# Linear attention and a four-expert merge: the first token tile and the second batch's attention moved into the seven-product block schedule

## The chip, the core and the metric

The kernel runs on one NeuronCore of a Trainium2 chip. Its engines work through queues of their own, in order: TensorE (PE in the profile) for matrix products, VectorE (DVE), ScalarE (ACT), GpSimd (POOL), and SyncE (SP), which here only issues transfers. PE writes to PSUM, which has eight banks of 512 float32 for each of 128 partitions; ACT and DVE read it. The metric is the device time of one execution in microseconds (us); lower is better. Eight executions of the kernel before had a median of 514.97 us (513.4 to 515.87).

## The reference

```python
phi = lambda x: where(x > 0, x, exp(x) - 1) + 1        # q, k, v: (8, 8, 576, 64)
q_p, k_p = phi(q), phi(k)
kv  = einsum('bhsd,bhse->bhde', k_p, v)
num = einsum('bhsd,bhde->bhse', q_p, kv)
den = einsum('bhsd,bhd->bhs', q_p, k_p.sum(2))[..., None] + 1e-06
x   = (num / den).transpose(0, 2, 1, 3).reshape(4608, 512)

p   = probs / (probs.sum(-1, keepdims=True) + 1e-09)   # (4608, 4)
out = 0
for e in range(4):
    out += p[:, e:e+1] * (maximum(x @ w1[e], 0) @ w2[e])   # w1 512x1024, w2 1024x512
```

All inputs are float32. The kernel computes in float16 with float32 sums.

## The kernel before

**Tiles.** Each batch has 576 tokens. The first 512 of batch j make token tile j (0 to 7); the 64 left over of all eight batches (the "lefts": `rl`, `kl`, `vl`, `ql`, `xl`) make tile 8. A unit (j, e) is one tile through one expert: layer 1 (512 to 1024, relu) and layer 2 (1024 to 512, scaled by the token's probability and added into `acc` by `add_acc`). There are 36 units.

**Two ways to do a unit.** The plain way (`layer1_group` L468, `layer2_part` L522) uses 32 matmuls of 512 columns for each layer. The block way splits each product of matrices 2 by 2 and uses seven half-size products instead of eight: `Block` (L659) does half of a unit's layer 1 in the products p1, p2, p6, p7, p5, p4, p3, each of 4 matmuls of 256 columns, so that a unit's layer 1 is 56 such matmuls; `layer2_product` (L591) does layer 2 in 14 steps of 4 matmuls. The block way needs sums beforehand: of the weights (`weight_sums` L549 for w1 and `weight_sums2` L563 for w2, four DVE operations each per expert, the fourth overwriting a quarter of the weight), of the tokens (`token_sum` L635, four POOL operations per tile into `tt`) and of the hidden values (`hidden_sum` L576, eight POOL operations per unit into `hs`). A block also takes five ACT operations (a copy `pe`, copies `u2` and `u3`, two relus) and two DVE operations (`add_relu` L656, from c22 and p3).

Before, the five units (0,0) to (0,3) and (1,0) are done the plain way and the 31 others in blocks.

**Attention of a batch** (`class Batch` L206). Loads of q, k and v in quarters of 2 heads (`load`, 256 KB) and of the lefts (`load_left`, 64 KB); phi of q and k (`phi_act` on ACT, `phi_dve` on DVE), cast of v (`vcast`), the products k'v (`kv`, ACT copies into `kvz`), the transposes of q' (`pe_qT` on PE with an ACT or DVE copy, or `dma_qT` by a transfer), the quotients (`nd`, `norm` on DVE), and the transposes of x into `xT` (`pe_xT` or `dma_xT`). Batches 0 and 1 take phi in one ACT and two DVE operations; later ones take two ACT operations (1+x, and exp into PSUM) and one DVE operation.

**Order.** Everything is in a manual schedule: each engine works in the order in which the program issues. First comes batch 0's attention, with the GpSimd queue issuing all weights (`load_w` L163: w1 and w2 of expert 0, then of 1, 2, 3, each in halves of 512 KB as float16) and after them batch 1's lefts and quarters (L827 to L830). Then the plain units of tile 0 run as a list of pieces (L891 to L906); `steps` (L855) lays batch 1's attention among the pieces of expert 2's end and expert 3. Then follows layer 1 of (1,0), also plain, and from L928 on the slot loop (L979): in each slot one product of the present or the previous block, and between them what is put at positions in slots: layer 2 products (`L2AT`, `L2ORD`), hidden sums (`HSUM`), and the attention of the next batch (`batch_steps` L740, positions in `ATTN`). Batch 2's attention, which runs beside tile 1, has a table of positions of its own, `ATTN[0]`, packed into 41 slots; the others use `ATTN[1]`, spread over 53. Eight weight sums for experts 2 and 3 lie in tile 1 (`WS2`).

**PSUM.** The tags `s`, `e`, `b` and `py` have two banks each. Blocks use `b` and `e`, layer 2 uses `py`. The attention's PSUM tiles (`aps` L156) take `s` and `e` in turn while tile 0 runs, and `s` alone afterwards (L921). A layer 2 step writes one half of a `py` bank (`run` or `side`).

**Buffers.** `rawb` has six buffers (NRAW) for quarters in flight; `rl` has one.

Of the kernel before, what the change touches and what calls it, by code (L numbers as in the profile page):

```python
# [19 lines left out]
CFG = {  # L20
    "ATTN": (
        dict(
            v=(0.3, 1.0, 3.2, 13.0),
            k=(0.6, 3.0, 6.7, 8.2),
            kd=(5.8, 6.8, 6.8, 9.5),
            lv=6.1,
            lk=9.7,
            lkd=12.0,
            kv=(13.6, 15.8),
            q=(16.1, 17.6, 19.1, 20.5),  # L30
            qd=(16.1, 18.4, 21.0, 22.6),
            lq=23.8,
            lqd=24.3,
            qT=23.8,
            nd=(32.8, 33.3, 34.1, 34.5, 38.2, 38.5),
            nl=41.4,
# [18 lines left out]
    "WS2": (6.6, 9.6, 26.1, 27.5, 25.7, 30.2, 37.6, 43.0),  # L55
# [4 lines left out]
    "TSUM1": (-1.2, 0.1, 0.4, 0.8),  # L60
# [4 lines left out]
def kernel(  # L65
# [11 lines left out]
    ATTN, WS2, HSUM, L2ORD, L2AT, TSUM, TSUM1 = (  # L77
        CFG[x] for x in ("ATTN", "WS2", "HSUM", "L2ORD", "L2AT", "TSUM", "TSUM1")
    )
# [34 lines left out]

    NB2 = 1
# [47 lines left out]
    def load_w(e, r):  # L163

        if e == 0 and r < 4:
            fs = slice(r * F // 4, (r + 1) * F // 4)
            nc.gpsimd.dma_start(out=w1_sb[e][:, :, fs], in_=w1_src[e, :, :, fs])
        elif r < 2 and e > 0:
            ds = slice(r * 2, r * 2 + 2)
            nc.gpsimd.dma_start(out=w1_sb[e][:, ds], in_=w1_src[e, :, ds])  # L170
        else:
            fs = slice(r % 2 * 4, r % 2 * 4 + 4)
            nc.gpsimd.dma_start(out=w2_sb[e][:, fs], in_=w2_src[e, :, fs])
# [32 lines left out]
    class Batch:  # L206
# [5 lines left out]
        def load_left(self, *names, eng=nc.sync):  # L212
            b = self.b
            if "k" in names:
                self.rl = praw.tile([P, 3, HG, D], FP32, tag="rawl", bufs=1, name="rl")
            for i, (name, src) in enumerate((("k", k), ("v", v), ("q", q))):
                for u in range(2):
                    if name in names:
                        eng.dma_start(
                            out=self.rl[u * HP : (u + 1) * HP, i],  # L220
                            in_=src[b, u * HG : (u + 1) * HG, SM:S].rearrange(
                                "h r d -> r h d"
                            ),
                        )

        def load(self, name, i, eng=nc.sync, home=None):
# [9 lines left out]
            else:  # L236
                t = pm.tile(shape, FP32, tag=home, bufs=2 if home == "u2" else 1, name="rawu")
# [6 lines left out]
        def alloc(self):  # L244
            self.kp = pa.tile([P, CM, H, D], FP16, tag="kp", bufs=1, name="kp")
            self.vp = pa.tile([P, CM, H, DE], FP16, tag="vp", bufs=1, name="vp")
            nc.gpsimd.memset(self.vp[:, :, :, D:DE], 1.0 / SX)
            self.vl = pa.tile([P, HG, DE], FP16, tag="vl", bufs=1, name="vl")
            nc.gpsimd.memset(self.vl[:, :, D:DE], 1.0 / SX)
            if self.b < 2:  # L250
# [3 lines left out]
            if self.b < 2:  # L254
                self.x = pm.tile([P, NPAIR, CM, P], FP16, tag="tt", bufs=2, name="x_sb")
            self.xl = pa.tile([P, 2, P], FP16, tag="xsl", bufs=1, name="x_sl")
            if self.b < 2:
# [9 lines left out]
        def phi_act(self, name, i):  # L267

            if self.b >= 2 and (name, i) == ("q", 0):
# [3 lines left out]
            if self.b >= 2:  # L273
# [8 lines left out]
        def phi_dve(self, name, i):  # L282
            src, dst, ee = self.ph.pop((name, i))
            dst, ee = (a.rearrange("p c h d -> p c (h d)") for a in (dst, ee))
            if self.b >= 2:
# [14 lines left out]
        def left_act(self, *names):  # L300

            for name in names:
# [8 lines left out]
                if self.b >= 2:  # L311
# [13 lines left out]
        def left_dve(self, name):  # L325
            src, el, parts = self.ph.pop("l" + name)
            for us, dst in parts:
                if self.b >= 2:
# [22 lines left out]
        def dma_qTl(self):  # L351
            for u in range(2):
# [4 lines left out]
                )  # L357

# [45 lines left out]
        def nd(self, i0, n):  # L404

            if i0 == 0 and self.b >= 2:
# [20 lines left out]
        def nd_left(self):  # L427
# [11 lines left out]
            for u in range(2):  # L439
# [151 lines left out]
    def layer2_product(j, e, hT, hss, p, i):  # L591


        if p == 2:
            pys[i] = new_py()
        run, side = pys[i][:, 0:DH], pys[i][:, DH:Dm]
# [5 lines left out]
            1: (run, lambda k: hT[k // 2][:, k % 2, 0, ts], w[:, lo, 0:DH], False),  # L602
# [32 lines left out]
    def token_sum(j, i):  # L635
# [7 lines left out]
        nc.gpsimd.tensor_tensor(out=t[:, i], in0=a, in1=b, op=AO.subtract)  # L643
# [100 lines left out]
    def batch_steps(bt, nxt, put, at, at_next):  # L744

        mine = order_of(at)
        later = mine + (order_of(at_next) if nxt is not None else [])

# [4 lines left out]
        def load_left():  # L753
            if nxt is not None:
                nxt.load_left("k", "v", "q")
# [7 lines left out]
        put(min(at["v"][0], at["k"][0]) - 0.01, bt.alloc)  # L763
        for m, (n, i) in enumerate(mine):
            if n == "v":
                put(at[n][i], bt.vcast, i)
                put(at[n][i] + 1, load, m + NRAW)
            else:
                put(at[n][i], bt.phi_act, n, i)
                put(at[n + "d"][i], bt.phi_dve, n, i)  # L770
                put(at[n][i] + 1, load, m + NRAW)
# [7 lines left out]
        put(at["lqd"] + 2, bt.dma_qTl)  # L779
        put(at["qT"], bt.dma_qT)  # L780
        for i in range(6):
            put(at["nd"][i], numerators, 3 * i, min(3, NPAIR * CM - 3 * i))
# [12 lines left out]
    with tc.manual_schedule(  # L795
        engines={ENG.PE, ENG.Activation, ENG.DVE, ENG.SP, ENG.Pool}
    ):
        b0.alloc()
        homes = ["h"] * 4 + [None] * NRAW + ["u2", "u3"]
# [22 lines left out]
        for r in range(6):  # L822
            load_w(0, r)
        for e in range(1, E):
            for r in range(4):
                load_w(e, r)
        b1.load_left("k", "v", "q", eng=nc.gpsimd)  # L827
        homes = [None] * NRAW + ["u2", "u3", "u2"] + [None] * 3
        for (n, i), home in zip(ORDER, homes):
            b1.load(n, i, nc.gpsimd, home=home)  # L830
# [24 lines left out]
        steps = [  # L855
            (1, b0.left_q),
            (2, emit_probs),
            (4, b0.dma_qTl),
            (22, b0.nd_left),
            (36, b1.alloc),  # L860
            (46, b1.phi, "q", 0),
            (46, b1.phi, "q", 1),
            (47, b1.left_kv),
            (48, b1.phi, "k", 0),
            (48, b1.phi, "k", 1),
            (49, b1.pe_qT, 0),
            (50, b1.pe_qT, 1),
            (50, b1.vcast, 0),
            (50, b1.vcast, 1),
            (52, b1.kv, 0),  # L870
            (53, b1.phi, "q", 2),
            (53, b1.phi, "q", 3),
            (54, b1.nd_pair, 0),
            (55, b1.phi, "k", 2),
            (55, b1.phi, "k", 3),
            (56, b1.nd_pair, 1),
            (56, b1.vcast, 2),
            (57, b1.pe_qT, 2, nc.scalar),
            (57, b1.vcast, 3),
            (58, b1.pe_xT, 0),  # L880
            (59, b1.pe_qT, 3, nc.scalar),
            (60, b1.kv, 2, 1),
            (60, b1.pe_xT, 1),
            (61, b1.kv, 3, 1),
            (62, b1.nd_pair, 2),
            (63, b1.nd_pair, 3),
        ]
        early = {(1, 1 + 2 * i): (0, i) for i in range(3)}
        early.update({(2, 1 + 2 * i): (1, i) for i in range(4)})
        done = 0  # L890
        pieces = unit(0, 0, hT, phs) + [g for e in range(1, E) for g in unit(0, e)]  # L891
        for i, g in enumerate(pieces):
            g[0](*g[1:])

            e, r = divmod(i, 16)
            if (e, r) in ((2, 14), (2, 15), (3, 1)):
                weight_sums(3, (r + 2) % 4 if e == 2 else 2)
            if r in (9, 11, 13) and e < 3:
                weight_sums(e, r // 2 - 4)
            elif r == 15 and e in (1, 2):  # L900
                weight_sums(e, 3)
            elif r in (1, 3, 5, 7) and (e, r) in early:
                weight_sums2(*early[e, r])
            while done < len(steps) and i >= steps[done][0]:
                steps[done][1](*steps[done][2:])
                done += 1  # L906

        hT = [new_h(), new_h()]
        phs = [layer1_group(1, 0, 0, hT, None, range(0, 2))]
        phs.append(layer1_group(1, 0, 1, hT, None, range(0, 2)))  # L910
        b1.pe_xT(2)
        phs.append(layer1_group(1, 0, 2, hT, None, range(0, 2)))
        b1.pe_xT(3)
        b1.left_q()
        for n, i in order_of(ATTN[0])[0:NRAW]:
            bts[2].load(n, i)
        bts[2].load_left("k", "v", "q")
        b1.dma_qTl()
        for i in range(4):
            token_sum(1, i)  # L920
        turn["aps"], turn["ph"] = ["s"], ["e"]  # L921
        for g in layer1(1, 0, hT, phs):
            g[0](*g[1:])
        weight_sums(0, 3)
        weight_sums(E - 1, 3)


        NSLOT, LAG = 7, 6  # L928
        units = [(j, e) for j in range(1, NTILES) for e in range(E) if (j, e) > (1, 0)]
        nslots = 2 * NSLOT * len(units)  # L930
# [5 lines left out]
        blocks = []  # L936
        for i, g in enumerate(layer2(1, 0, hT, 4)):
            put_at(i * (2 * NSLOT + LAG) // 16 + 0.5, *g)
        put_at(2 * NSLOT + LAG + 0.5, weight_sums2, 0, 3)
        for n, (j, e) in enumerate(units):  # L940
            hT, hss = [None, None], [[None] * 4, [None] * 4]
            blocks += [Block(j, e, d, hT) for d in range(2)]
            at = 2 * NSLOT * (n + 1) + LAG

            def hsum(d, i, hT=hT, hss=hss):
                hidden_sum(hT[d], hss[d], i)

            for d in range(2):
                for i in range(4):
                    put_at(at + HSUM[d][i], hsum, d, i)  # L950
            for m in range(14):
                put_at(at + L2AT[m], layer2_product, j, e, hT, hss, L2ORD[m // 2], m % 2)
# [71 lines left out]
```

## Time and profile before

| | |
|---|---|
| median of eight executions | 514.97 us (513.4 to 515.87) |
| profiled execution | 513.4 us, span 511.6 us, mean TensorE clock 0.991 |
| PE busy | 489.0 us (96%) |
| DVE, POOL, ACT busy | 365.7, 345.7, 323.8 us |
| data moved by transfers | 54.29 MB, mean 106 GB/s |
| time to landing of a 512 KB weight half | 10.6 to 20.8 us, in a queue |

A line of the timeline gives start and duration in us, engine, line of the kernel, operation, what it writes and reads, its shape, how many instructions are merged, and in brackets how long its engine stood idle before it and what ended that. SPq and POOLq are the issuing of transfers. The end of a matmul is modelled with its latency: four matmuls of 256 columns show as 0.60 us but the next four start 0.44 us after them, so lengths of PE work are taken here between starts.

### The profile page before, as it was taken

What the parts mean: (1) busy time and instruction counts of PE and PEld (TensorE: products, weight loads), DVE (VectorE), ACT (ScalarE), POOL (GpSimd) and SP (SyncE); (2) the same over time, 40 slices, a digit from 0 to 9 for tenths busy, and PEclk for the clock granted to TensorE, in tenths of its full rate; (3) what the DMA queues carried; (4) which work ended last, traced back from release to release, by engine and by line L of the source; (5) the groups of instructions that cost most, each with busy time, mean ns of one, the idle gap of its engine ahead of it and who ended that gap; (6) DMA issues with size and microseconds to landing.
All of it is one profiled execution on the core that took longest, in us unless ns stands there. A gap on an engine that the chain in (4) does not pass through costs nothing.

```text
span 511.6 us, 11256 instructions
## 1 busy us (share of the span) xinstructions
PE 489.0 (96%) x4199; PEld 397.1 (78%) x4199; DVE 365.7 (71%) x787; ACT 323.8 (63%) x647; POOL 345.7 (68%) x340
## 2 busy tenths in 40 slices
PE   6899978889999999999999999999999999999994
PEld 3444444567888888898989898888988888888883
DVE  5725585459986878687868796889688756775674
ACT  5753485994689568955895589559954464446520
POOL 2622523055887697769866986698669877987781
PEclk9999999999999999999999999999999999999999
DMA  8999944646444424442445244623231020001003
GB/s 239 209 208 207 218 151 167 180 117 108 64 150 162 97 63 136 148 108 63 140 145 118 50 142 145 108 51 113 84 68 27 2 83 1 1 21 65 1 1 83
DMA packets 80935, 54.29 MB, mean 106 GB/s; under 512 B 46224, under 2 KB 73872, under 8 KB 80880
## 3 DMA queue, kind: packets, MB, share of 16 engines
q1 hardware_dynamic: 71760, 41.64, 31.2%
q0 software_dynamic: 9120, 11.93, 12.0%
q8 instruction: 33, 0.54, 0.4%
q14 instruction: 22, 0.18, 0.1%
HBM read 45.16 MB, written 9.44 MB: 107 GB/s over the span
## 4 chain that ended last, share of the span: by engine, by line
PE 80%; DVE 9%; ACT 5%; DMA 2%; issue 2%; SPq 1%; POOL 0%; DVEq 0%; ACTq 0%; POOLq 0%
PE py L611 35%; PE pb L673 19%; PE pe L673 14%; PE ph L472 5%; PE py L527 5%; DVE acc L518 3%; DVE x_sb L397 2%; PE psum_kv L374 1%; DMA qT<-qp 1%; PE psum_nd L414 1%; DVE h L657 1%; DMA rl<-in_v_dram 1%; ACT u L684 1%; SPq L239 1%; ACT psum_ee L279 1%
## 5 line engine op out<-in xcount | busy, mean ns | idle before, releaser
L518 DVE SCALAR_TENSOR_TENSOR acc<-py,p_sb,acc 128x256 f32<-128x256 f32 (+1 forms) x390 | 184.0, 488 | 62.0 <-PE py L611 48.9
L583 POOL TENSOR_TENSOR hs<-h 128x512 f16<-128x512 f16 x62 | 71.9, 1160 | 67.7 <-DVE h L657 67.7
L657 DVE CUSTOM_DVE_ANT_0 h<-pe,u 128x512 f16<-128x512 f32 x124 | 85.4, 689 | 36.2 <-PE pe L673 18.7
L673 PEld LDWEIGHTS <-w 128*128 128x128 f16 x992 | 96.4, 98 | 16.3 <-issue 2.9
L611 PEld LDWEIGHTS <-h 128*128 128x128 f16 x992 | 97.4, 98 | 14.9 <-issue 2.7
L611 PE MATMUL py<-w,h 128*128 128x256 f16 x744 | 107.4, 274 | 0.7 <-DVE acc L518 0.2
L585 POOL TENSOR_TENSOR hs<-hs,h 128x512 f16<-128x512 f16 x62 | 71.6, 1155 | 24.9 <-PE py L611 22.4
L684 ACT COPY u<-pb 128x512 f32<-128x512 f32 x124 | 73.0, 589 | 22.5 <-PE pb L673 20.2
L611 PEld LDWEIGHTS <-hs 128*128 128x128 f16 x744 | 71.8, 98 | 11.4 <-issue 2.9
L673 PEld LDWEIGHTS <-s 128*128 128x128 f16 x744 | 72.5, 98 | 9.3
L611 PE MATMUL py<-t,hs 128*128 128x256 f16 x496 | 74.4, 272 | 1.2 <-DVE acc L518 1.0
L673 PE MATMUL pb<-tt,w 128*128 128x256 f16 x496 | 74.7, 273 | 0.9 <-ACT u L684 0.9
L589 POOL TENSOR_TENSOR hs<-h,hs 128x512 f16<-128x512 f16 x62 | 71.7, 1156 | 3.2 <-PE py L611 3.2
L587 POOL TENSOR_TENSOR h<-h 128x512 f16<-128x512 f16 x62 | 72.1, 1162 | 0.0
L699 ACT ACTIVATE h<-pe 128x512 f16<-128x512 f32 x62 | 37.0, 597 | 53.1 <-PE pe L673 52.6
L693 ACT COPY pe<-pb 128x512 f32<-128x512 f32 x62 | 35.9, 579 | 46.8 <-PE pb L673 43.2
L527 PE MATMUL py<-w,h 128*128 128x512 f16 x160 | 38.4, 379 | 0.8 <-DVE acc L518 0.8
L472 PE MATMUL ph<-xT,w 128*128 128x512 f16 x160 | 37.1, 379 | 0.8 <-ACT xT L451 0.7
L717 ACT ACTIVATE h<-pb 128x512 f16<-128x512 f32 x62 | 36.9, 596 | 1.4 <-PE pb L673 1.2
L673 PE MATMUL pe<-tt,s 128*128 128x256 f16 x248 | 37.3, 273 | 0.0
L673 PE MATMUL pb<-tt,s 128*128 128x256 f16 x248 | 37.2, 273 | 0.0
L516 ACT ACTIVATE acc<-py,p_sb 128x256 f32<-128x256 f32 (+1 forms) x64 | 31.4, 507 | 7.5 <-PE py L527 4.2
(102 smaller groups left out, 634.7 us busy)
## 6 DMA issues: line engine op xcount, KB each, us to landing
out_dram<-acc SPq DMA_DIRECT2D x32, 256.0 KB, 2.4
w<-in_moe_w_dram POOLq DMA_DIRECT2D x14, 512.0 KB, 19.6
rawb<-in_v_dram SPq DMA_DIRECT2D x26, 256.0 KB, 2.9
rawb<-in_q_dram SPq DMA_DIRECT2D x26, 256.0 KB, 3.0
rawb<-in_k_dram SPq DMA_DIRECT2D x26, 256.0 KB, 2.8
w<-in_moe_w_dram POOLq DMA_DIRECT2D x4, 256.0 KB, 8.0
rawb<-in_v_dram POOLq DMA_DIRECT2D x4, 256.0 KB, 4.4
out_dram<-acc SPq DMA_DIRECT2D x8, 128.0 KB, 2.4
```

Source lines behind the costliest of these rows:

```text
L472: nc.tensor.matmul(out=ph, lhsT=w1_sb[e][:, dc, fj * P : (fj + 1) * P], rhs=xT_of(j)[:, dc], start=(dc == 0), stop=(dc == DC - 1),)
L518: nc.vector.scalar_tensor_tensor(out=acc, in0=ps, scalar=pscal, in1=acc, op0=AO.mult, op1=AO.add)
L527: nc.tensor.matmul(out=py, lhsT=rows(hT, fj)[:, ns * P : (ns + 1) * P], rhs=w2_sb[e][:, fj, :], start=(fj == 0), stop=(fj == FC - 1),)
L583: nc.gpsimd.tensor_tensor(out=hs[0], in0=a21, in1=a22, op=AO.add)
L585: nc.gpsimd.tensor_tensor(out=hs[1], in0=hs[0], in1=a11, op=AO.subtract)
L587: nc.gpsimd.tensor_tensor(out=a21, in0=a11, in1=a21, op=AO.subtract)
L589: nc.gpsimd.tensor_tensor(out=hs[3], in0=a12, in1=hs[1], op=AO.subtract)
L611: nc.tensor.matmul(out=ps, lhsT=lhsT(k), rhs=rhs[:, k], start=first and k == 0, stop=k == FH - 1, skip_group_check=True,)
L657: nc.vector._custom_dve(TENSOR_ADD_SAT, out=out, in0=ps, in1=u, s0=BIG, s1=0.0)
L673: nc.tensor.matmul(out=ps[:, kk], lhsT=lk(kc), rhs=rhs[:, kc], start=first and kk == 0 and kc == 0, stop=kc == 1, skip_group_check=True,)
L684: nc.scalar.copy(u, self.b)
L699: nc.scalar.activation(self.h[:, :, 0, 0:NH], self.e5, AF.Relu)
```

## The change

Layer 1 of (0,1), (0,2), (0,3) and (1,0) and layer 2 of (1,0) are done in blocks; layer 2 of tile 0 stays plain, and (0,0) stays plain altogether. Tile 0's token sums are four DVE operations. The slot loop is gone: every step, from the second half of (0,0)'s layer 1 on, has a position in `CFG`, and the sorted list is issued. Batch 1's attention gets positions 20 to 56 beside the blocks of (0,2) and (0,3), takes phi as the later batches do (two ACT operations, one DVE), keeps its q' and x in the buffers of `kp` and `vp`, and uses only the two `s` banks for all its PSUM tiles. The lefts of batches 0 and 1 are transposed by PE (`pe_qTl`, `pe_xl`) and not by transfers. Batch 2's attention uses the table that the later batches use. The GpSimd queue issues weights and batch 1's quarters and lefts mixed, in the order `DMA`. In the last unit, layer 2's `run` and `side` halves get banks of their own from `b` and `e`, and its steps come in another order.

```diff
 CFG = {
+    "DMA": ('w100', 'w101', 'w102', 'w103', 'w110', 'w200', 'w201', 'w111', 'lk0', 'w210', 'w121', 'w120', 'w211', 'lv0', 'lk1', 'v0', 'lv1', 'w221', 'w220', 'w131', 'lq0', 'k0', 'w130', 'k1', 'v1', 'v2', 'k2', 'lq1', 'k3', 'v3', 'q3', 'q2', 'q0', 'q1', 'w231', 'w230'),
+    "BLK": (-1.0, 6.0, 13.0, 21.0, 28.0, 35.0, 53.0),
+    "L1P": (-40.4, -39.9, -23.1, -21.7, -21.5, -19.6, -16.2, -14.3),
+    "L2P": ((-14.0, -13.2, -12.6, -12.6, -11.8, -5.4, -4.5, -2.9, -1.4, 0.3, 3.9, 5.5, 9.1, 11.6, 16.0, 16.8), (20.4, 21.5, 22.7, 23.0, 23.4, 23.9, 23.9, 24.6, 24.6, 24.7, 27.2, 27.7, 27.8, 28.4, 28.4, 34.6), (37.0, 37.1, 38.8, 40.1, 40.6, 41.8, 42.5, 43.5, 44.6, 45.0, 45.4, 45.9, 46.4, 47.5, 53.3, 55.2), (49.2, 49.8, 55.6, 55.7, 56.7, 57.2, 58.6, 59.2, 61.3, 61.4, 62.1, 62.7, 64.9, 65.9, 67.0, 71.8)),
+    "TS0": (-37.7, -33.9, -28.9, -12.1),
+    "WS1": ((-3.3, -1.0, 7.3, 14.1), (-8.2, -3.1, -1.2, -1.2), (15.2, 16.0, 23.6, 15.3), (27.1, 27.6, 29.5, 27.2)),
+    "WS2": ((6.9, 13.3, 43.3, 50.6), (24.5, 29.9, 35.6, 38.6), (51.7, 61.8, 74.1, 59.6), (63.9, 66.1, 70.6, 80.0)),
     "ATTN": (
         dict(
...
+            v=(22.5, 27.0, 27.3, 31.4),
+            k=(21.5, 26.8, 28.0, 28.3),
+            kd=(26.2, 29.1, 29.3, 29.4),
+            lv=24.5,
+            lk=20.4,
+            lkd=26.4,
+            kv=(31.8, 33.5),
+            q=(34.0, 36.3, 36.6, 39.3),
+            qd=(36.4, 37.8, 38.6, 43.0),
+            lq=28.6,
+            lqd=29.4,
+            qt=(42.4, 43.2, 43.5, 43.6),
+            nd=(43.1, 44.9, 45.7, 46.8),
+            xt=(44.1, 48.8, 49.5, 49.8),
+            qtl=35.1,
+            nl=53.0,
+            xl=55.6,
+            next=(8.5, 35.8, 36.8, 39.6, 43.2, 49.6),
         ),
...
+    def load_first():
+        parts = [x for x in CFG["DMA"] if x[0] in "vkq"]
+        homes = dict(zip(parts, [None] * NRAW + ["acc"] + [None] * 5))
+        b1.alloc_left()
+        for x in CFG["DMA"]:
+            if x[0] == "w":
+                load_w(*map(int, x[1:]))
+            elif x[0] == "l":
+                b1.load_left(x[1], eng=nc.gpsimd, us=(int(x[2]),))
+            else:
+                b1.load(x[0], int(x[1]), nc.gpsimd, home=homes[x])
...
-            if self.b >= 2:
+            if self.b >= 1:
                 nc.scalar.activation(dst.rearrange("p c h d -> p h c d"), src, AF.Identity, bias=1.0)
                 ee = aps([P, HQ * CM * D], FP32, "psum_ee")
...
+        def pe_qTl(self):
+            ps = aps([P, 2, P], FP16, "psum_ql")
+            for a in range(2):
+                nc.tensor.transpose(out=ps[:, a], in_=self.ql[:, 2 * a : 2 * a + 2], identity=identh)
+            for u in range(2):
+                us = slice(u * HP, (u + 1) * HP)
+                nc.scalar.copy(out=self.qTl[:, :, u, us], in_=ps[:, :, us])
...
-        run, side = pys[i][:, 0:DH], pys[i][:, DH:Dm]
+        if (j, e) == (NTILES - 1, E - 1):
+            if p == 2:
+                pys[i] = [ppm.tile([P, DH], FP32, tag=tag, bufs=2, name=f"p{tag}") for tag in ("b", "e")]
+            run, side = pys[i]
+        else:
+            if p == 2:
+                pys[i] = new_py()
+            run, side = pys[i][:, 0:DH], pys[i][:, DH:Dm]
...
-        for r in range(6):
-            load_w(0, r)
-        for e in range(1, E):
-            for r in range(4):
-                load_w(e, r)
-        b1.load_left("k", "v", "q", eng=nc.gpsimd)
...
+        load_first()
...
-        steps = [
-            (1, b0.left_q),
...
+        turn["aps"] = ["s"]
...
+        def put_block(at, *g):
+            bl = Block(*g)
+            for pos, name in ((0, "p1"), (3, "p2"), (5, "p6"), (8, "p7"), (9, "p5"), (9.1, "c22"), (11, "p4"), (13, "p3")):
+                put_at(at + pos, getattr(bl, name))
...
+        for e in range(E):
+            h0 = hT if e == 0 else [None, None]
+            for d in range(2) if e else ():
+                put_block(CFG["BLK"][2 * e - 2 + d], 0, e, d, h0)
+            for i, pos in enumerate(CFG["L2P"][e]):
+                put_at(pos, layer2_part, 0, e, i // 4, h0, i % 4, 4)
+            for i in range(4):
+                put_at(CFG["WS1"][e][i], weight_sums, e, i)
+                put_at(CFG["WS2"][e][i], weight_sums2, e, i)
+        base = CFG["BLK"][6]
...
+            order = L2ORD if n < len(units) - 1 else (2, 1, 5, 6, 3, 7, 4)
...
+                batch_steps(bts[j + 1], nxt, put, ATTN[j > 0], ATTN[1])
...
         work.sort(key=lambda w: w[0:2])
+        for _, _, g in work:
+            g[0](*g[1:])
```

In `DMA`, `w1er` is part r of expert e's w1 and `w2er` of its w2; `lk0` is a half of the lefts of k; `k0` is quarter 0 of k.

## The prediction

> **What bounds the kernel now.** I read the page first: PE is busy 96%, so its work and its gaps are the time. Then the windows, to find the gaps; then the timeline there.
>
> ```profile
> PE   6899978889999999999999999999999999999994
> ...
> 19.40:61.90 42.50, 42.20 (x205) 19.53 (x206) 19.49 (x38) 19.05 (x33) 13.70 (x20) 1.00 1.15 206
> 62.00:91.60 29.60, 25.46 (x166) 13.26 (x165) 19.68 (x51) 19.30 (x40) 10.20 (x16) 1.00 0.54 180
> 91.70:134.80 43.10, 38.08 (x305) 28.66 (x304) 31.32 (x63) 31.24 (x63) 20.42 (x17) 0.96 0.54 114
> 186.80:238.20 51.40, 51.40 (x490) 46.05 (x489) 40.95 (x90) 37.99 (x78) 40.26 (x39) 1.00 0.42 114
> ```
>
> After each stretch and its length come busy us (and instructions) of PE, PEld, DVE, ACT, POOL, then clock, DMA share, GB/s. From 187 on PE has no gap. Up to 62 it hardly has one, but transfers run at a share over 1: weights come as fast as they can. Between 62 and 135 lies the loss.
>
> How much, I count from starts. Four 256-column matmuls follow each other at 0.437 us, four of 512 at 0.864, a small one (128 or 130 columns) takes 0.0575. From 62.0 to 91.6 PE does 98 wide and 68 small ones, 25.1 of 29.6 us: 4.5 lost. The first block of (1,1) starts at 91.73, of (2,0) at 134.83:
>
> ```profile
> 91.73 0.60 PE L673 MATMUL pb<-xT,w 128*128 128x256 f16 x4
> 134.83 0.60 PE L673 MATMUL pb<-xT,w 128*128 128x256 f16 x4
> 186.83 0.60 PE L673 MATMUL pb<-xT,w 128*128 128x256 f16 x4
> 238.25 0.60 PE L673 MATMUL pb<-xT,w 128*128 128x256 f16 x4
> ```
>
> Between the first two lie 152 block matmuls (16.6), (1,0)'s plain layer 2 (6.9), 19 layer 2 steps (8.3) and attention (2.5): 34.3 of 43.1, 8.8 lost. Tile 2 takes 52.0, tile 3 51.4, and their work is 51.4. So 13.3 us can be had here.
>
> **The change, part by part.** *Less PE work.* A layer is 32 x 0.216 = 6.91 plain, 56 x 0.109 = 6.11 in blocks. Five layers change: 4.0 us less. Eight small transposes are new: 0.5 more.
>
> *The new transfer order.* The GpSimd queue lands its transfers one after another:
>
> ```profile
> 30.33 0.70 POOL L170 DMA_DIRECT2D w<-in_moe_w_dram  x1 [2.01 <-DMA w<-in_moe_w_dram]
> 33.02 0.71 POOL L170 DMA_DIRECT2D w<-in_moe_w_dram  x1 [1.99 <-DMA w<-in_moe_w_dram]
> 38.05 0.74 POOL L173 DMA_DIRECT2D w<-in_moe_w_dram  x1 [1.79 <-DMA w<-in_moe_w_dram]
> ```
>
> Each issue plus its time to landing gives, after expert 0's w1, halves at 24.7, 26.4, 29.1, 31.8, 35.2, 37.7, 40.4, 42.8, 45.3, 48.4, 51.0, 53.4, 56.0 and 58.9. Batch 1's quarters then land 0.95 apart, its lefts about 0.25. In the new order v0, five lefts and k0 stand before the twelfth half: k0 lands at 51.0 + 2 x 0.95 + 5 x 0.25 = 54.1 (ends: 51.0 if they ride along free, 57.5 if a quarter costs as much as a half, 2.65; I take the quarters' own rows), w130 at 56.5, k1 to k3 at 57.5 to 61.5, q1 at 66, w230 at 71.5. On its queue lk0 must wait until batch 0's left q is read (near 24); four halves are then under way until 31.8, so nothing runs dry.
>
> *PE up to there.* (0,0) runs as before to 27.6. Waits for w201 (0.6), for batch 0's leftover quotient (0.9) and for w120, before the first block of (0,2) (1.5, to 40.5), leave PE at 53.3 with nothing to do before w130. ACT comes to batch 1's k0 near 46.5 and stands there until 54.1, with two relus behind it that must free a `b` bank before (0,3) can start.
>
> *ACT from 54.1.* Its queue from k0 to the first transpose copy of q' holds 34 operations of 512 columns and nine small ones. In the trace such operations start 0.513 apart (nine from 92.43 to 97.05), though each shows 0.6:
>
> ```profile
> 92.94 0.62 ACT L295 CAST vp<-rawb 128x512 f16<-128x512 f32 x1
> 93.46 0.63 ACT L274 ACTIVATE kp<-rawb 128x512 f16<-128x512 f32 x1
> 93.99 0.59 ACT L279 ACTIVATE psum_ee<-rawb 128x512 f32<-128x512 f32 x1
> 94.51 0.61 ACT L295 CAST vp<-rawb 128x512 f16<-128x512 f32 x1
> ```
>
> 34 x 0.513 + 2.8 for the small ones + 0.5 waiting for k2 is 20.7: the copy ends at 74.8. PE has 20.0 us of work between 56.5 and tile 1, and follows ACT. DVE has 25 us in the 30 (six `add_relu` at 0.69, seven phis at 0.69, ten weight sums at 0.69, five sums into `acc` at 0.74, eight quotients at 0.55), so it runs beside.
>
> *From 74.8 to tile 1.* What is left on PE hangs on that copy: 12 groups at 0.435 (5.2), ten attention groups at 0.23 (2.3), and the hand-overs quotient to DVE to transpose, 1.9. Tile 1 starts at 84.2.
>
> *The clock.* PE idles at half the time between 53 and 66. The trace shows what that can do: the clock was 0.50 from 113.2 to 116.6, after 3.4 us in which PE ran 1.3. A gap of 3.1 us (66.7 to 69.8) did nothing. One slow stretch costs 0 (PE waits for ACT anyway) to 1.7 us (half of 3.41); I take 0.7, since PE reaches the copies only 1.4 us early. So tile 1 starts at 84.9.
>
> ```profile
> 110.00:111.00 1.00, 0.00 (x1) 0.00 (x0) 0.17 (x1) 1.00 (x3) 0.00 (x0) 1.00 0.58 168
> 114.00:115.00 1.00, 1.00 (x7) 0.73 (x5) 0.65 (x2) 1.00 (x3) 1.00 (x2) 0.50 0.39 108
> ```
>
> The Trainium skill, "TensorE: Matmul & The Clock Gate", Why this matters for your kernels, speaks against the change: no gaps over about 3 us, since an idle window halves the clock. By it the wait for w130 (3.2 us) would cost a full 1.7 and the sum would be 1.0 us worse; in this trace such a gap cost nothing, and the row goes before.
>
> *Tile 1.* Work until (2,0): tile 0's rest (6.9), four layers less four products (22.7), 33 layer 2 steps (14.4), attention (2.7): 46.7. Batch 2 has the table of the later batches, whose tiles lose 0 to 0.6; I take 0.5 (ends 0 and the 8.8 of before). The weight sums here (seven, 4.8 us) replace layer 2 sums. (2,0) starts at 132.1, 2.7 earlier than 134.83. Tile 2 takes 51.4 and not 52.0: 0.6.
>
> *Beside other work:* tile 0's token sums on DVE (4 x 0.42, where DVE idled 11.4 us before 40.85); (1,0)'s hidden sums (8 x 1.16, where POOL idled 14.9 before 104.99); SyncE's two transposes gone at 24 and 92. Were that cover gone, they would cost 1.7, 9.3 and nothing.
>
> *The end.* Every pair of layer 2 steps takes 1.17 us, since the next step waits for DVE on the same bank:
>
> ```profile
> 502.15 1.33 PE L611 MATMUL py<-w,hs 128*128 128x256 f16 x8
> 503.32 1.33 PE L611 MATMUL py<-w,h 128*128 128x256 f16 x8
> 503.30 5.61 SPq L505 DMA_DIRECT2D out_dram<-acc  x8
> 505.86 0.48 DVE L518 SCALAR_TENSOR_TENSOR acc<-py,p_sb,acc 128x256 f32<-128x256 f32 x1 [0.25 <-PE py L611]
> ```
>
> With four banks DVE sets the pace, 14 x 0.46, and the last sum ends 1.7 earlier. But the eight stores follow each other for 5.61 us from the first, which needs step 3, and that needs the last hidden sum (501.26): 501.3 + 0.45 + 0.5, so stores begin at 502.3. The end gains 1.0.
>
> **Sum.** -2.7 - 0.6 - 1.0 = -4.3. On the profiled execution's 513.4 that is 509.1; it lies 1.57 under the median, so for the median 514.97 - 4.3 = **510.7 us**.
>
> **Rivals.**
> *A, slower: two PSUM banks for the whole attention.* Batch 1's 29 PSUM tiles go through two `s` banks in 30 us; before, they had four. Each hand-over that ACT's queue does not hide is paid in the chain. From 0.15 us each (4.3 / 29) the gain is gone; at 0.25, 7.2 us more, 517.9. For it: PE, ACT and DVE are all near full there. Against: later batches live on `s` alone without loss, but at 46 us a batch.
> *B, faster: ACT does not bind*, since PE's waits let it catch up: tile 1 starts at 56.5 + 20.0 = 76.5, 8.4 earlier: 502.3. For: ACT is busy 63% overall. Against: its queue order.
> *C: tile 1 loses half of its 8.8 again* (DVE 31 and ACT 31 of 43 us before did not prevent it): 4.4 more less 0.5, 514.6.
>
> **How the numbers follow.** Forecast 0.55, A 0.20, B 0.13, C 0.12. The forecast's own range is 507.5 to 514 (k0's and the clock's ends). For 8 in 10, 505 to 518 reaches from near B into A. About 0.2% (1 us) can be told from no change: faster 0.67, same 0.08, slower 0.25.
>
> **What would show it.** An ACT idle of 7 us before batch 1's phi of k0, ended by its landing near 54; ACT near full from there to 75; tile 1's first product near 85, tile 2's near 132, no gaps after; stores beginning 1 us after the last hidden sum. It is wrong if k0 lands elsewhere, if ACT has gaps after 54 (A), or if PE is full from 57 on (B).

## The result and the profile after

The changed kernel takes 511.54 us (median of 13 executions, 510.70 to 512.92) against 514.79 us (median of 38): a ratio of 0.9941 (0.9932 to 0.995), or 3.25 us less. The forecast was 510.7, 4.3 less. Its profiled execution is one of 511.54 us, with a span of 509.8. The profiled execution of the kernel before (513.40) equals the fastest of the 38, 1.39 us under their median: the two spans differ by 1.87 us only, and 1.87 + 1.39 is the 3.25, but for rounding. So the two traces locate 1.87 us of the gain; where the other 1.39 lies they do not show.

The page of the changed kernel, busy time by engine and PE's tenths in 40 slices:

```profile
PE 482.6 (95%) x4327; PEld 407.3 (80%) x4327; DVE 377.7 (74%) x800; ACT 336.1 (66%) x679; POOL 354.9 (70%) x339
...
PE   6788789899999999999999999999999999999994
```

Its windows (columns as in the prediction):

```profile
19.40:61.90 42.50, 34.96 (x224) 20.96 (x225) 26.12 (x51) 27.61 (x57) 19.62 (x28) 1.00 1.14 236
62.00:82.10 20.10, 18.44 (x160) 12.60 (x160) 17.03 (x37) 15.23 (x33) 0.00 (x0) 1.00 0.73 153
82.10:131.10 49.00, 47.44 (x422) 39.06 (x420) 39.28 (x79) 37.61 (x80) 36.00 (x32) 1.00 0.44 119
183.10:235.10 52.00, 51.78 (x490) 46.09 (x489) 41.10 (x90) 38.22 (x78) 40.63 (x37) 1.00 0.43 113
```

And the starts of (1,0), (2,0), (3,0) and (4,0) in its timeline:

```profile
82.15 0.38 PE L722 MATMUL pb<-xT,w 128*128 128x256 f16 x2
...
131.11 0.38 PE L722 MATMUL pb<-xT,w 128*128 128x256 f16 x2
...
183.12 0.38 PE L722 MATMUL pb<-xT,w 128*128 128x256 f16 x2
...
235.12 0.38 PE L722 MATMUL pb<-xT,w 128*128 128x256 f16 x2
```

Subtract the starts of the kernel before. (2,0) comes 3.72 us earlier (134.83 before), more than the 2.7 forecast. Then the lead melts: (3,0) 3.71, (4,0) 3.13, (5,0) 2.53, (6,0) 1.96, (7,0) 1.37, (8,0) 1.28, (8,3) 1.21. Tiles 3 to 6 each take 0.6 us more than before (3, 4 and 6 take 52.0 where they took 51.4), and tile 2 takes 52.0 as before. From (8,3) to the end 0.66 us is won (32.20 against 32.86). So -3.72 + 2.51 - 0.66 = -1.87.

**Where the later tiles lose.** The same place in tile 3, just after the first product of (3,1), first in the changed kernel, then in the one before:

```profile
195.50 0.60 PE L722 MATMUL pb<-xT,w 128*128 128x256 f16 x4
...
195.94 0.60 PE L660 MATMUL py<-w,h 128*128 128x256 f16 x4
...
196.23 0.87 DVE L562 SCALAR_TENSOR_TENSOR acc<-py,p_sb,acc 128x256 f32<-128x256 f32 x2
...
196.76 0.60 PE L660 MATMUL py<-t,hs 128*128 128x256 f16 x4 [0.22 <-DVE acc L562]
...
197.19 0.60 PE L722 MATMUL pb<-tt,w 128*128 128x256 f16 x4
```

```profile
199.06 0.60 PE L673 MATMUL pb<-xT,w 128*128 128x256 f16 x4
...
199.49 0.60 PE L611 MATMUL py<-w,h 128*128 128x256 f16 x4
...
200.01 0.60 PE L673 MATMUL pb<-tt,w 128*128 128x256 f16 x4
...
200.44 0.60 PE L611 MATMUL py<-t,hs 128*128 128x256 f16 x4
```

Before, a product stood between the two layer 2 steps and covered DVE's sums; now they stand back to back, and the second starts 0.82 us after the first instead of 0.44. The diff shows why: the slot loop issued a slot's product first and then everything placed in that slot. The sorted list breaks a tie by the order of insertion, and the layer 2 steps of a unit (positions 9.0 and 10.0 in `L2AT`) are inserted before the later units' products p7 and p5 with the same position.

**What tile 1 loses.** From its first product to (2,0) it takes 48.96 us for 46.59 us of work. Most of that is two waits of this kind:

```profile
93.07 0.63 ACT L301 ACTIVATE kp<-rawb 128x512 f16<-128x512 f32 x1
...
93.59 0.60 ACT L306 ACTIVATE psum_ee<-rawb 128x512 f32<-128x512 f32 x1
...
94.11 0.60 ACT L733 COPY u<-pb 128x512 f32<-128x512 f32 x1
...
94.76 0.60 PE L722 MATMUL pb<-tt,w 128*128 128x256 f16 x4 [0.83 <-ACT u L733]
```

The copy of (1,1)'s first product stands behind batch 2's phi of k3, and few layer 2 steps are there to cover it: between the first products of (1,1) and (1,2) PE does 22 layer 2 matmuls, in each unit of tile 2 it does 56.

### The profile page after: what moved, and what is told of

Read it like the earlier page. It is cut to its first block, busy times and chain, and to the rows that moved or that the text cites. A ratio compares the mean times of both kernels' runs of the same rounds, so it can differ in the third digit from the quotient of the medians.

```text
span 509.8 us, 11541 instructions
## 1 busy us (share of the span) xinstructions
PE 482.6 (95%) x4327; PEld 407.3 (80%) x4327; DVE 377.7 (74%) x800; ACT 336.1 (66%) x679; POOL 354.9 (70%) x339
## 4 chain that ended last, share of the span: by engine, by line
PE 78%; ACT 8%; DMA 8%; issue 2%; DVE 2%; SPq 1%; POOL 1%; ACTq 0%; DVEq 0%; POOLq 0%
PE py L660 36%; PE pb L722 21%; PE pe L722 16%; DMA w<-in_moe_w_dram 3%; DMA rawb<-in_k_dram 2%; PE psum_nd L458 1%; DVE acc L562 1%; DMA rawu<-in_v_dram 1%; ACT psum_ee L306 1%; DMA qT<-qp 1%; ACT vp L322 1%; PE psum_kv L418 1%; ACT u L733 1%; DMA rawb<-in_v_dram 1%; ACT kp L301 1%
## 5 line engine op out<-in xcount | busy, mean ns | idle before, releaser
L706 DVE CUSTOM_DVE_ANT_0 h<-pe,u 128x512 f16<-128x512 f32 x140 | 96.6, 690 | 50.1 <-PE pe L722 30.0
L722 PEld LDWEIGHTS <-w 128*128 128x128 f16 x1120 | 108.4, 98 | 20.9 <-issue 4.9
L733 ACT COPY u<-pb 128x512 f32<-128x512 f32 x140 | 82.5, 589 | 33.7 <-PE pb L722 31.6
L722 PEld LDWEIGHTS <-s 128*128 128x128 f16 x840 | 82.1, 98 | 13.9 <-DVE s L599 1.8
L722 PE MATMUL pb<-tt,w 128*128 128x256 f16 x560 | 84.0, 273 | 2.3 <-ACT u L733 2.3
L633 POOL TENSOR_TENSOR hs<-h,hs 128x512 f16<-128x512 f16 x64 | 74.3, 1162 | 6.4 <-PE py L660 5.4
L660 PE MATMUL py<-t,hs 128*128 128x256 f16 x496 | 74.3, 272 | 1.4 <-DVE acc L562 1.4
L631 POOL TENSOR_TENSOR h<-h 128x512 f16<-128x512 f16 x64 | 74.3, 1161 | 0.0
L748 ACT ACTIVATE h<-pe 128x512 f16<-128x512 f32 x70 | 41.8, 597 | 48.7 <-PE pe L722 46.3
L766 ACT ACTIVATE h<-pb 128x512 f16<-128x512 f32 x70 | 41.7, 596 | 3.5 <-PE pb L722 3.3
L722 PE MATMUL pb<-tt,s 128*128 128x256 f16 x280 | 42.0, 273 | 1.6 <-DVE s L599 1.6
L722 PE MATMUL pe<-xT,w 128*128 128x256 f16 x248 | 37.2, 272 | 1.3 <-ACT pe L742 1.3
L722 PE MATMUL pe<-xT,s 128*128 128x256 f16 x248 | 37.2, 273 | 0.0
```

Source lines behind the costliest of these rows:

```text
L631: nc.gpsimd.tensor_tensor(out=a21, in0=a11, in1=a21, op=AO.subtract)
L633: nc.gpsimd.tensor_tensor(out=hs[3], in0=a12, in1=hs[1], op=AO.subtract)
L660: nc.tensor.matmul(out=ps, lhsT=lhsT(k), rhs=rhs[:, k], start=first and k == 0, stop=k == FH - 1, skip_group_check=True,)
L706: nc.vector._custom_dve(TENSOR_ADD_SAT, out=out, in0=ps, in1=u, s0=BIG, s1=0.0)
L722: nc.tensor.matmul(out=ps[:, kk], lhsT=lk(kc), rhs=rhs[:, kc], start=first and kk == 0 and kc == 0, stop=kc == 1, skip_group_check=True,)
L733: nc.scalar.copy(u, self.b)
```

## The experiments

Theory: from the landing of k0 ACT's queue sets tile 1's start; the later tiles lose to the tie; tile 1 loses to ACT. "Stage one" below is the time from ACT's phi of k0 to tile 1's first product: 29.14 us in the changed kernel.

**1. Products first at equal positions** (on the changed kernel)

```diff
-            work.append((pos, len(work), g))
+            work.append((pos, 1, len(work), g))
-            for pos, name in (..., (9, "p5"), (9.1, "c22"), ...):
-                put_at(at + pos, getattr(bl, name))
+            for pos, name in (..., (9, "p5"), (9, "c22"), ...):
+                work.append((at + pos, 0, len(work), (getattr(bl, name),)))
-        work.sort(key=lambda w: w[0:2])
+        work.sort(key=lambda w: w[0:3])
...
```

> The changed kernel with one rule of its sorted list altered: where a block product and another step have the same position, the product goes first, as in the slot loop of the kernel before, and c22 follows p5 directly. From (2,0) on, TensorE then gets its products and layer 2 steps in the very sequence of the kernel before. Theory (order): in the changed kernel two layer 2 steps stand back to back where they share a position with p7 or p5, and the second waits for DVE's sum (gaps of 0.49 us at 144.26, 196.26, 248.27). Tiles 2 to 6 take 51.4 us again (52.1 for the one with a late transfer) instead of 52.0 (52.7), 5 x 0.6 = 3.0 us; tile 1 gains 0.4, the end 0.5 (the last hidden sum came 0.48 later after (8,3)'s start than before). 511.5 - 3.9 = 507.6 us. Rival (DVE late in any order: with the second batch's later load positions its queue is full there): the periods stay 52.0 and the time within 0.5 us of 511.5.

Measured: 508.04 us, ratio to the kernel before 0.987 (0.985 to 0.989). The same place in tile 3, and the starts of (2,0), (3,0), (4,0):

```profile
195.15 0.60 PE L722 MATMUL pb<-xT,w 128*128 128x256 f16 x4
195.59 0.60 PE L660 MATMUL py<-w,h 128*128 128x256 f16 x4
196.12 0.60 PE L722 MATMUL pb<-tt,w 128*128 128x256 f16 x4
196.55 0.60 PE L660 MATMUL py<-t,hs 128*128 128x256 f16 x4
```

```profile
131.49 0.49 PE L722 MATMUL pb<-xT,w 128*128 128x256 f16 x3
...
182.93 0.60 PE L722 MATMUL pb<-xT,w 128*128 128x256 f16 x4
...
234.36 0.60 PE L722 MATMUL pb<-xT,w 128*128 128x256 f16 x4
```

Tiles take 51.4 again; (2,0) to (8,0) is 306.81 us, not 309.70, and from (8,3) to the end 31.77, not 32.20. Tile 1 gained nothing (48.96 again; 0.4 was expected). The order theory holds: the tie cost 3.5 us by the medians, as much as the whole measured gain, and 3.3 us by the trace from (2,0) to the end.

**2. The last unit's edit alone, on the kernel before**

```diff
+        if (j, e) == (NTILES - 1, E - 1):
+            if p == 2:
+                pys[i] = [ppm.tile([P, DH], FP32, tag=tag, bufs=2, name=f"p{tag}") for tag in ("b", "e")]
+            run, side = pys[i]
...
+            order = L2ORD if n < len(units) - 1 else (2, 1, 5, 6, 3, 7, 4)
```

> The kernel before with the last unit's edit alone: run and side halves in banks of their own, step order 2, 1, 5, 6, 3, 7, 4. Theory (the prediction's term): stores begin 1.0 us after the last hidden sum, the end gains 1.0 us, 514.8 becomes 513.8. Other: what the changed kernel's profile shows against the one before, from (8,3)'s start to the end, is 32.24 against 32.83, 0.6 us, and 514.2. Rival: the last hidden sum and eight stores one after another set the end, 514.8, no change. Its trace up to (8,3) is also a second profile of the kernel before: if the first was a lucky one, tile starts here lie about 1.5 us later, and the place of it is seen.

Measured: 513.05 us, ratio 0.9968 (0.9954 to 0.9981), 1.0 to 2.4 us less. In the trace 31.60 us from (8,3) to the end against 32.86: 1.26. Stores begin 1.0 us after the last hidden sum, as forecast (502.85 after 501.85). Its tiles start 0.3 to 0.6 us later than in the first profile of before, not 1.5: at most part of what made that execution fast lies ahead of the last unit. The half-speed stretch lay elsewhere, at 70 to 75 us, not 113 to 117.

**3 and 4. More work for ACT, more work for DVE** (on the changed kernel)

```diff
...
+        for pos in (29.5, 30.5, 31.5, 32.5, 33.6, 34.9):
+            put_at(pos, nc.scalar.copy, scr, xT_of(0)[:, 0, 0:256])
```

> The changed kernel with six ACT copies of 256 columns more, spread over batch 1's attention between its quarter k2 and its q quarters (about 58 to 68 us). They add some 6 x 0.33 = 2.0 us of work to ACT's queue and to nothing else; their result is not used. Theory (from the landing of k0 ACT's queue sets the start of tile 1): tile 1's first product goes from 82.15 to 84.1, and the time from 511.5 to 513.5. Rival B (ACT does not bind, TensorE or DVE do): first product within 0.5 us of 82.2, time 511.5 to 512.0.

```diff
+        for pos in (29.5, 31.5, 33.6):
+            put_at(pos, weight_sums2, 2, 0)
```

> The changed kernel with three DVE operations more in the same stretch: expert 2's first layer 2 weight sum is computed three times more, 3 x 0.69 = 2.07 us, each into the place where it belongs. Theory (ACT's queue binds, DVE runs beside): tile 1's first product moves by 0 to 0.7 us from 82.15, time 511.5 to 512.2. Rival (DVE binds as well: 16.9 of 20 us busy between 62 and 82, and the product of k' and v waited 2.2 us for its phi): first product at 84.2, time 513.6.

Measured: 513.17 us (ratio 0.9968, 0.9953 to 0.9983) with more on ACT, 511.90 (0.9945, 0.9924 to 0.9967) with more on DVE. ACT's first operation on k0 and its first copy of transposed q', with more on ACT:

```profile
52.08 0.63 ACT L302 ACTIVATE kp<-rawb 128x512 f16<-128x512 f32 x1 [3.06 <-DMA rawb<-in_k_dram]
...
73.38 0.63 ACT L410 COPY qT<-psum_qT 128x512 f16<-128x512 f16 x1
```

and in the changed kernel:

```profile
53.01 0.63 ACT L301 ACTIVATE kp<-rawb 128x512 f16<-128x512 f32 x1 [3.31 <-DMA rawb<-in_k_dram]
...
72.29 0.64 ACT L409 COPY qT<-psum_qT 128x512 f16<-128x512 f16 x1
```

21.30 against 19.28, and stage one is 31.16 against 29.14: both 2.02 more, the whole work added. (k0 came 0.93 earlier in that execution, so the absolute start moved by 1.09 only.) With more on DVE, stage one is 29.92; that execution had a half-speed stretch in it, as had experiment 1 with 29.86, whose stage one is otherwise like the changed kernel's but for the ties, so 2.07 us of DVE work cost next to nothing; none of its executions (511.38 to 512.80) reached the 513.6 of the rival. ACT binds there, DVE does not.

**5 and 6. k0 one place later, one place earlier in the transfers** (on the changed kernel)

```diff
-'w131', 'lq0', 'k0', 'w130', 'k1',
+'w131', 'lq0', 'w130', 'k0', 'k1',
```

> The changed kernel with two transfers exchanged: k0 after the weight half w130 and not before it. k0 lands one half later, some 2.4 us. Theory (from k0's landing ACT's queue sets tile 1's start, and with it the time): ACT's phi of k0 at 55.2, not 52.1 to 53.0; tile 1's first product 2.0 to 2.5 later, 84.4; time 511.5 + 2.2 = 513.7. Rival (the landing is not on the path, since ACT's queue has slack later): first product within 0.5 us, 511.5 to 512.

```diff
-'w131', 'lq0', 'k0', 'w130', 'k1',
+'k0', 'w131', 'lq0', 'w130', 'k1',
```

> The changed kernel with k0 one place earlier, before w131 (and lq0). k0 lands some 2.4 us earlier, near 50.5; w131 and w130 land 0.95 later. Theory: ACT, free from 49.7, does k0 at 50.5; then it needs TensorE's last blocks of (0,2) for the two relus and (0,3)'s first product, which has its weights at 56.7, so that only part is won: tile 1's first product 0 to 1.0 earlier, time 510.5 to 511.5. If the landing of k0 alone sets the start: 2.4 earlier, 509.1. If the weights set it: 0.9 later, 512.4.

Measured: 514.59 us late (ratio 1.0002, 0.9992 to 1.0012), above the forecast of 513.7; 511.28 early (0.9932, 0.9913 to 0.995). Late:

```profile
55.20 0.63 ACT L301 ACTIVATE kp<-rawb 128x512 f16<-128x512 f32 x1 [5.58 <-DMA rawb<-in_k_dram]
```

Tile 1's first product comes at 85.19, 3.04 later: 2.19 is k0's delay, the other 0.85 goes with a half-speed stretch at 64 to 67 us. One transfer in the wrong place eats the whole gain. Early brings nothing clear: phi of k0 starts at 49.51, but the copy of (0,3)'s first product and the landing of k1 come next, each with a wait, and the stage is 31.74. The first product at 81.25, 0.90 earlier, only shows that this whole execution ran ahead (a copy of ACT's in (0,2), at 45.83 and not 46.88, came 1.05 earlier as well). In the changed kernel k1 had landed at 56.09 and ACT took it up at 56.31; with k0 out of the way ACT waits for k1 itself, so that only these 0.22 us are to be won. From k1's phi to tile 1 it is 25.84 us there and 25.93 here.

**7. One ACT operation less for q1 to q3** (on the changed kernel)

```diff
+        def one_act(self, name, i):
+            return self.b == 1 and name == "q" and i > 0
...
-            if self.b >= 1:
+            if self.b >= 1 and not self.one_act(name, i):
...
```

> The changed kernel with phi of batch 1's quarters q1, q2 and q3 in the form of batch 0: one ACT operation (exp) and two DVE operations on the loaded values, not two and one. ACT has 3 x 0.52 = 1.6 us less in its queue between 68 and 72, DVE 3 x 0.69 = 2.1 us more. Theory (ACT's queue sets the start; 2.0 us more on ACT moved tile 1's start, counted from k0's phi, by 2.0, and 2.1 us more on DVE by 0.8): -1.6 + 0.8 = -0.8 us, first product 28.3 after k0's phi (29.1 in the changed kernel), time 510.7. Rival (what ACT loses DVE gains at the same price, since the quotients and the sums wait there): 0 to +0.5, time 511.5 to 512.

Measured: 511.78 us (ratio 0.994, 0.9926 to 0.9953), no gain. Stage one is 29.57, with a half-speed stretch, 0.3 under experiment 1. DVE's new form even costs less than assumed (two operations of 0.42 us for one of 0.69, so 0.15 more for a quarter). But ACT, with 1.6 us less to do, now waits 0.71 us for PE's first transposes of q' and 1.12 for the next ones, and PE waits 1.08 for DVE ahead of those (0.69 in the changed kernel). At the end of the chain the hand-overs between the three engines bind; the rival was right on the time, though not for the price that it gave.

**8. Two of batch 2's phis moved behind a copy** (on experiment 1)

```diff
+                at2 = dict(ATTN[1], k=(1.3, 2.7, 5.7, 14.3), q=(21.3, 24.3, 27.0, 29.3))
+                batch_steps(bts[j + 1], nxt, put, (ATTN[0], at2, ATTN[1])[min(j, 2)], ATTN[1])
```

> The kernel of the equal-positions run (products first; 508.0 us), with two of batch 2's phi steps in tile 1 moved behind the first product of a block: k3 from 11.5 to 14.3, q0 from 18.8 to 21.3 (and q1 from 23.6 to 24.3). In the changed kernel TensorE waited 0.83 and 0.68 us in (1,1) for ACT's copy u2 (94.76 and 100.22), which stood in ACT's queue behind the two phi operations of k3 and of q0; that is most of what tile 1 lost (48.96 us from its first product to (2,0), for 46.6 of work). Theory (queue order): the copies come first, both waits go, first product of tile 1 to (2,0) 47.5, time 506.6. Rival (ACT is full from 92 to 110, 17.8 of 18.4 us, so the wait only moves to the next copy): 48.5 to 49.0, time 507.6 to 508.2.

Measured: 509.61 us (ratio 0.9897, 0.9883 to 0.9911), slower than experiment 1 and above both forecasts. Tile 1 takes 49.39 us. PE's waits there of 0.5 us and more:

```profile
103.20 0.60 PE L722 MATMUL pb<-tt,w 128*128 128x256 f16 x4 [0.67 <-ACT u L733]
106.31 0.60 PE L660 MATMUL py<-w,h 128*128 128x256 f16 x4 [0.77 <-ACT acc L560]
```

The waits went from where they were and came up later. Moving two steps does not take the loss away. (Of the 1.57 us to experiment 1, tile 1 explains 0.43; in the profiled execution another 0.95 lay in stage one, 30.81 us, with a half-speed stretch twice as long.)

**9. Batch 2's q work spread later** (on experiment 1)

```diff
+                at2 = dict(
+                    ATTN[1], q=(25.5, 30.0, 33.0, 35.0), qd=(27.5, 32.0, 34.5, 36.5), lq=37.0, lqd=39.5,
+                    qT=38.5, nd=(42.0, 43.0, 44.0, 45.5, 47.0, 49.0),
+                )
...
```

> The kernel of the equal-positions run (508.0 us) with batch 2's q work spread later in tile 1: q at 25.5, 30, 33, 35 (not 18.8, 23.6, 27, 29.3), its leftovers at 37, q' transposes at 38.5, quotients from 42 to 49. That takes some ten ACT operations, 5 us, out of 92 to 110 us, where ACT was busy 17.8 of 18.4 us, and puts them where it was busy 11.5 of 23. Theory (ACT's capacity there is what tile 1 loses): first product of tile 1 to (2,0) 47.4 instead of 48.96, time 506.5. Rival (the loss is the order of single steps, and any order has some): 48.5 to 49.4, time 507.6 to 508.5. If the later q' makes (2,0) wait for x: over 50, time over 509.

Measured: 511.52 us (ratio 0.9949, 0.9932 to 0.9967), 3.5 slower than experiment 1; the third case came, tile 1 takes 51.69 us. (1,1) gained 0.92 us (10.94 instead of 11.86), ACT being relieved as meant, and (1,2) and (1,3) lost 3.7:

```profile
114.40 1.03 PE L660 MATMUL py<-w,h 128*128 128x256 f16 x8 [0.83 <-ACT acc L560]
120.11 0.34 PE L458 MATMUL psum_nd<-kvz,qT 128*128 128x130 f16 x3 [1.18 <-DMA qT<-qp]
```

ACT's capacity does cost tile 1 something at its beginning, but the later q' then collides with `acc` sums and its transfer. What else would bring tile 1 to its 46.6 us stays open.

**10. Filler matmuls in PE's wait** (on experiment 1)

```diff
+        put_at(31.79, warm, 8)
```

> The kernel of the equal-positions run (508.0 us) with eight matmuls of 512 columns on TensorE (1.73 us, result not used) just ahead of batch 1's first product of k' and v, where TensorE stands 2.2 us after a wait of 1.0. In the executions profiled so far with a half-speed stretch (about 3.3 us near 60 to 66) tile 1's first product came 29.86 us after ACT's phi of k0, in the one without it 29.14. Theory (the clock halves after TensorE has idled most of some 4 us, though no single gap is over 2.3): no half-speed stretch between 58 and 68, 29.1 us from k0's phi to tile 1, time 507.3. Rival (the clock goes down for another reason): the stretch stays, 29.8 us, 508.0. If the filler delays the product of k' and v: 30 us and more, 508.5.

Measured: 506.98 us, ratio 0.9858 (0.9839 to 0.9878), the lowest median of all, faster than the kernel before and the changed one; its interval overlaps that of experiment 1. The clock is the column after POOL. Experiment 1, then this one:

```profile
60.00:62.00 2.00, 0.43 (x5) 0.43 (x5) 1.65 (x4) 2.00 (x6) 1.04 (x2) 0.74 1.06 297
62.00:64.00 2.00, 2.00 (x15) 1.63 (x13) 1.67 (x3) 1.68 (x5) 0.00 (x0) 0.50 1.01 209
64.00:66.00 2.00, 2.00 (x21) 1.58 (x20) 0.44 (x1) 1.71 (x5) 0.00 (x0) 0.90 1.23 202
```

```profile
60.00:62.00 2.00, 1.53 (x10) 0.66 (x9) 1.57 (x3) 2.00 (x6) 1.39 (x2) 1.00 0.79 254
62.00:64.00 2.00, 2.00 (x28) 1.82 (x27) 1.96 (x4) 1.96 (x6) 0.00 (x0) 1.00 0.99 236
```

Stage one is 29.01 us, and no half-speed stretch is left there (one at 11 to 15 us, ahead of batch 1's attention, is). The difference of the medians to experiment 1, 1.06 us, is about as large as the scatter of five executions; one profiled execution of each gives 0.85 for stage one.

**11 and 12. All together, and without the spread**: experiments 1, 6, 9 and 10 in one kernel, then 1, 6 and 10.

> Products first at equal positions, batch 2's q work spread later, the eight filler matmuls, and k0 ahead of w131 in the transfers (which brought tile 1's first product 0.9 us forward where no half-speed stretch disturbed). If the four effects add up: 508.0 - 1.5 - 0.7 - 0.5 = 505.3 us. If those of stage one overlap (the filler fills what k0's earlier landing makes): 506.0. If ACT in tile 1 only takes up what is won ahead of it: 507.5.

> Products first at equal positions, the eight filler matmuls, and k0 ahead of w131; batch 2's table as in the changed kernel. If the two earlier findings on stage one add up (k0 one place earlier: tile 1's first product 0.7 to 0.9 us earlier where no half-speed stretch disturbed; filler: 507.0 us): first product at 81.3, time 506.2. If what is won ahead of tile 1 is lost in it again, because ACT is full there whenever it begins: first product at 81.3, but first product to (2,0) 49.5 and more, time 507.0.

Measured: 510.02 us (ratio 0.9908, 0.9887 to 0.9929) and 507.54 (0.9866, 0.9841 to 0.989), both above all their forecasts. The first pays for the spread again (tile 1 50.94). The second is no faster than experiment 10. ACT in it:

```profile
55.18 0.58 ACT L733 COPY u<-pb 128x512 f32<-128x512 f32 x1 [1.22 <-PE pb L722]
56.28 0.63 ACT L301 ACTIVATE kp<-rawb 128x512 f16<-128x512 f32 x1 [0.52 <-DMA rawb<-in_k_dram]
```

k0's phi began at 50.29 there, 2.74 earlier than in experiment 10, but ACT then waited for k1, whose phi began at 56.28 against 56.33; the first product came at 82.03 against 82.04. So k0 earlier wins nothing as long as k1 stays where it is.

## Why the prediction was right, and where it was not

The time fell 0.84 us from the forecast, and part of that is luck, since errors cancelled. Between the two profiled executions (2,0) came 1.0 us earlier than forecast, the later tiles ended 3.1 worse and the end 0.3 worse: 1.87 us won, not 4.3. That the medians lie 3.25 apart, nearer to the forecast, comes with the 1.39 us that no trace locates.

**Stage one: right in its mechanism, 2.75 us too late.** ACT idled until k0's landing, then had no gap to 72.9, as forecast; experiments 3 and 5 show that this chain sets tile 1's start. k0 came at 53.0 and not 54.1 (1.1); the chain to the end of the first copy took 19.9 and not 20.7 (0.8); copy to tile 1 took 9.2, not 9.4 (0.2); the clock term of 0.7 did not fall due in the profiled execution, though it did in others (below). ACT's idle time was 3.3 us, not 7: PE had waited 1.6 us for a weight sum (46.24), so ACT's work on (0,2) came later. Partly for the same reason the forecast wait of 3.2 us for w130 did not come: PE reached (0,3) at 55.79, when w130 had landed (55.27). How the 3.72 us at (2,0) divide among the block schedule, the transfer order and the form of phi no run shows; experiment 5 shows only that one transfer in another place takes back 2.2.

**Tile 1: its loss was mis-sized.** Work 46.7 forecast, 46.6 measured; lost 2.4 and not 0.5. "Later tiles lose 0 to 0.6" was the wrong row: by the traces they have layer 2 steps to put between products throughout, tile 1 has few beside (1,1). That this is the reason was not tested; experiments 8 and 9 did not win the loss back. (2,0) at 131.1, not 132.1: the 2.75 less 1.8.

**Tiles 2 to 7: the step that failed.** "Tile 2 takes 51.4 and not 52.0" and "no gaps after" took for granted that a slot loop and a sorted list with the same positions give the same sequence. They do not where positions are equal, and 2.5 us went there instead of -0.6; experiment 1 brings them back.

**The end: right in its mechanism.** 1.0 forecast, 0.66 measured in the changed kernel, where the last hidden sum came 0.48 later after (8,3)'s start; 1.26 alone on the kernel before, 1.09 with the ties mended.

**The base.** The gaps were read from an execution 1.39 us faster than the median of 38, and the sum was set against a median. Between medians that came out nearer than between the profiled executions; why, the runs do not show.

**Two misread rows.** Halves landed at 27.3, 30.0 and 32.7 us, where the prediction has 26.4, 29.1 and 31.8: it took a median over two transfers for the time of one. Its sum uses only the 51.0, which is right. Its gap of 3.1 us is taken up under the clock, below.

**Rivals.** A, the hand-over of two `s` banks: not paid, ACT has no gap to 72.9. B, ACT does not bind: refuted by experiment 3. C, tile 1 loses 4.4: it lost 2.4.

## What to carry to other kernels

When a hand-written order is produced in a new way (a loop becomes a sorted list), compare the sequences of the steady part instruction by instruction on each engine; here equal positions cost 3.5 us, as much as the whole change gained. What bounds a stage is found by adding 2 us of unused work to one engine and measuring from the event that starts the chain, not from the start of the run, since the event itself moves by a microsecond from execution to execution. Work taken off the binding engine near the end of the chain won nothing here, since the hand-overs behind it bound next.

## What the runs showed of the clock

Between 57 and 64 us PE stands twice, 0.6 to 1.5 us and 2.2 us by the profile's waits, with four matmuls between. In the nine profiled executions of the changed kernel and its variants without the filler, the clock then went to half in experiments 1, 4, 5, 7, 8 and 9 and did not in the changed kernel or in experiments 3 and 6. In experiment 1 the lost share (0.26, 0.50 and 0.10 of 2 us) is a stretch of 3.4 us at half speed, in experiment 8 it is one of 6.8. It goes with 0.7 us more in stage one (29.86 against 29.14), the doubled one with 1.7 (30.81).

The least busy 3.41 us there hold 0.60 to 0.62 us of PE work in each of the nine, with the filler 2.1 and more; the changed kernel, then experiment 10:

```profile
58.14:61.55 3.41, 0.60 (x4) 0.38 (x4) 2.57 (x5) 3.41 (x8) 3.24 (x5) 1.00 0.88 287
56.08:59.49 3.41, 2.10 (x16) 1.46 (x15) 3.22 (x5) 3.41 (x8) 2.22 (x4) 1.00 0.86 251
```

With the filler no stretch came there in three of three. That the filler is the reason is likely and not shown: three of nine had none without it either, and two of the three also have k0 earlier. The mean clock of the executions that were not profiled (0.990 to 0.993 in experiment 10, 0.991 to 0.995 in experiment 1) does not tell them apart.

The prediction's "gap of 3.1 us (66.7 to 69.8)" that "did nothing" is 2.62 us by the wait in its row. In experiment 2, where the order is the same up to there, the same wait was followed by a half-speed stretch from 70.9 to 74.3:

```profile
69.36 0.39 PE L374 MATMUL psum_kv<-vp,kp 128*128 128x130 f16 x4 [2.62 <-POOL vl L321]
...
72.00:74.00 2.00, 2.00 (x9) 0.98 (x8) 1.39 (x5) 1.56 (x3) 0.00 (x0) 0.50 0.04 8
```

So such a gap is not free; it has a chance of costing something.

The Trainium skill, "TensorE: Matmul & The Clock Gate", Part 1: The HAM clock gate (the "warmup" mystery), says that activity is judged over a free-running window of some 3.4 us, which does not start with the kernel. The lengths, 3.4 and twice that, agree, and so does a stretch that comes in some executions of the same wait. The rule that the prediction weighed, no gap over about 3 us, is too mild for this case: no wait there was over 2.21 us, and still a stretch followed two waits near each other in six executions of nine.
